# Stores of z, of the kept rows and of the first w1 and w2 operands issued by ScalarE in place of GpSimd

## The chip, the cores and the metric

The kernel runs on one core of a Trainium2 chip. The metric is the device time of one execution in microseconds, the median of several runs. Before the change the median of 3 runs is 1948.03 us (1947.04 to 1948.57).

The engines are named as in the profile: PE is TensorE (PEld its weight loads), DVE VectorE, ACT ScalarE, POOL GpSimd and SP SyncE. An engine carries out its own instructions in order. A DMA transfer is an instruction on one engine's queue (SPq, ACTq, POOL); the transfer itself then runs beside the engines.

## What is computed

A block of a network with modulation, an FNet mixing and an MLP, in float32, with S = 2048 rows and D = 1024 columns, F = 3584:

```
mod = (silu(c) @ w_mod)  ->  sa, ca, ga, sb, cb, gb
h = layernorm(x) * (1 + ca) + sa
a = h @ dft_hid_re^T ; b = h @ dft_hid_im^T
x = x + ga * (dft_seq_re @ a - dft_seq_im @ b)
h = layernorm(x) * (1 + cb) + sb
x = x + gb * (gelu(layernorm(h) @ w1 + b1) @ w2 + b2)
```

## The kernel before

Every matrix product is carried out in fp16 with each float32 operand split into a high and a low half (ScalarE makes the high half, VectorE subtracts it for the low half) and three products per pair (`PASSES`). All large products use Winograd's (Strassen's) scheme of seven products for a 2 by 2 block of matrices; `ORDER` = 0, 1, 2, 4, 3, 6, 5 is their order. Their operands are sums and differences of quarters, split into halves, and many are stored to DRAM once and loaded again later.

The stages, by the time in the profile:

- To about 617 us: normalising x, the product along the sequence, first plain (line 1272), then Winograd (line 1324). Its result u is split and stored to DRAM (line 906, issued by ScalarE), as are the operands s (line 774) and dc (line 985).
- 617 to 918 us, `gemm2`, line 1561: the product along the hidden dimension for eight blocks of 256 rows (b = 0 to 7). One product is two pieces of 12 matmuls. An eviction of a finished product to SBUF is done by ScalarE (line 1577) or VectorE (line 1583); a later product of the same bank goes on accumulating after it. Beside this VectorE and ScalarE do the two layer norms of the blocks (`ln_tasks`), whose result with gb*b2 added is the "kept" row block that is stored to the output (line 1427). The normalised rows are transposed on TensorE (line 1463) and `z_tasks` makes from them the seven operands z of a block (high half line 401, low half line 411, sums line 426), which are stored to zc in DRAM (line 1495). Weight operands of the MLP are made meanwhile: w1 for its first three groups g (line 1160) and w2 for its first pair v = 0 (line 1207), stored to DRAM through two staging buffers.
- 918 us to the end: the MLP, 28 groups of the first layer (`gemm3`, line 1755; 12 matmuls a product, evicted by line 1777 on ScalarE and 1781 on VectorE, gelu in line 1774) and 14 pairs of the second (`gemm4`, line 1864; evicted by line 1900 on ScalarE in the first pair of each half and by line 1910 on VectorE). The z of blocks 6 and 7 and the kept rows of block 7 are still being made in the first groups, from about 937 to 1000 us. SP loads the stored operands back: zc at line 1503, the stored w1 at lines 1736, 1741 and 2050, the first w2 at line 2072.

The order of all instructions is planned by the program itself when it is built. Work is cut into `Task`s with an engine, a modelled cost in us, dependencies and a due time, put in streams, and `fill_to` and `pick` hand out the next task by modelled clocks of the engines (`clk`) and modelled times at which results are there (`done`). `need` and `emitted` force what must come first. A store goes through `store`. By default it is a task of the kind "st": it takes no engine's modelled time, is issued 0.3 us (`BEHIND`) after what it stores is ready, plus the lag of its stream, and lands after `LANDS["st"]` = 4.0 us, also for z. If its ring is in the table `SYNC`, the store is a task of ScalarE with the cost given there, is put in a stream of its own with a due time ahead of all others, and lands after `SLAND` = 5.5 us:

```
        if ring in SYNC:
            t.eng, t.cost = "act", SYNC[ring]
            LANDS[t.key] = SLAND
        push(f"q_{ring}" if ring in SYNC else ring, tag or f"st_{ring}", [t], -1e6)

    SYNC = {"u": 0.5, "s": 0.8, "d": 0.8}
    SLAND = 5.5
```

The rings here are "z" (the operands z, with five or four staging places a block), "x2" (the kept rows) and "w1" (the staged w1 and w2). A task that writes a staging place again depends on the store that last read it (`slot`, `reuse`).

GpSimd's other work in these stages is the all-reduce over partitions in the norms of the weights (line 1064) and, late in the kernel, the stores that add to the output (lines 1938 and 1963).

Of the kernel before, what the change touches and what calls it, by code (L numbers as in the profile page):

```python
# [36 lines left out]
def kernel(ctx, tc, x, cre, cim, dre, dim, w1, b1, w2, b2, c, wm, out):  # L37
# [13 lines left out]
    pe, act, dve, gp, sp = nc.tensor, nc.scalar, nc.vector, nc.gpsimd, nc.sync  # L51
# [144 lines left out]
    w1_d = [dram.tile([P, 7, 2, 512], F16, tag=f"w1_{g}", name=f"w1_{g}") for g in range(14)]  # L196
    w2_d = [dram.tile([P, 7, 2, 2, 512], F16, tag=f"w2_{v}", name=f"w2_{v}") for v in range(7)]
# [67 lines left out]
    def push(stream, tag, tasks, due=0.0):  # L265
        for t in tasks:
            t.tag, t.due, t.lag = tag, due, LAGS.get(stream, LAT)
            streams.setdefault(f"st_{stream}" if t.eng == "st" else stream, deque()).append(t)

    def store(ring, n, f, after, tag=None):  # L270

        t = Task("st", 0.0, f, [after], ("st", ring, n))
        if ring in SYNC:
            t.eng, t.cost = "act", SYNC[ring]
            LANDS[t.key] = SLAND
        push(f"q_{ring}" if ring in SYNC else ring, tag or f"st_{ring}", [t], -1e6)

    SYNC = {"u": 0.5, "s": 0.8, "d": 0.8}
    SLAND = 5.5

    def slot(ring, n):
# [649 lines left out]
    dst = [0]  # L931
# [152 lines left out]
    def two1(g, n):  # L1084

        return at(raw1_at(g, n), 1024).rearrange("p (s x) -> p s x", s=2)
# [38 lines left out]
    def w1_tasks(g):  # L1125
        def after(n):
            if g < 3:
                return
            if n < 2:
                load_w1(g + 1, n + 2)  # L1130
            else:
                load_w1(g + 2, n - 2)

        s, p, sid = g % 2, g % NPAIR, {}

        def q(n):
            return two1(g, n[0]) if isinstance(n, tuple) else raw1(g, n)

        def span(m):
            return slice(m[0], m[1] + 1) if isinstance(m, tuple) else slice(m, m + 1)  # L1140

        def outs(m):
            v, n = w1c[:, span(m), s], 1 + isinstance(m, tuple)
            if g > 4:
                reuse("w1k", (g - 2, m))
            if g < 3:
                stage[0] += 1
                reuse("w1", stage[0] - 2)
                sid[m] = stage[0]
                v = at((172, 176)[stage[0] % 2], 1024 * n, F16).rearrange("p (m a x) -> p m a x", m=n, a=2)  # L1150
            return v[:, :, 0], v[:, :, 1], v

        def q1(n):
            t = q(n)
            return t if isinstance(n, tuple) else t.rearrange("p (m x) -> p m x", m=1)

        def post(m, o):

            ring, n, tag = ("w1", sid[m], "st_w1") if g < 3 else ("w1k", (g, m), None)
            store(ring, n, lambda: (gp if g < 3 else sp).dma_start(w1_d[g][:, span(m)], o[2]), ("w1", g, span(m).start), tag)  # L1160

        return left_tasks(
            q1, outs, s1c[:, p : p + 1], False, lambda n: ("raw1", g, n), lambda m: ("w1", g, m), after, post,
            (lambda m: ("g3", g - 2, m)) if g > 2 else None,
            (lambda m: slot("w1", lambda: stage[0] - 1)) if g < 3 else None,
        )
# [24 lines left out]
    def w2_tasks(v):  # L1191
        u, sid = v % 7, {}

        def outs(m):
            w = w2c[:, m]
            if v > 1:
                reuse("w2k", (v - 1, m))
            if v == 0:
                stage[0] += 1
                reuse("w1", stage[0] - 2)  # L1200
                sid[m] = stage[0]
                w = at((172, 176)[stage[0] % 2], 2048, F16).rearrange("p (s a x) -> p s a x", s=2, a=2)
            return w[:, :, 0], w[:, :, 1], w

        def post(m, o):
            ring, n, tag = ("w1", sid[m], "st_w2") if v == 0 else ("w2k", (v, m), None)
            store(ring, n, lambda: (sp if v else gp).dma_start(w2_d[v][:, m], o[2]), ("w2", v, m), tag)

        return right_tasks(
            [raw2(v, q) for q in range(4)], outs, s2c[:, u : u + 1], 1024,  # L1210
            lambda n: ("raw2g" if v == 6 else "raw2", v, n), lambda m: ("w2", v, m), (lambda q: load_w2(v + 1, q)) if v else None, post,
            (lambda m: ("g4", v - 1, m)) if v else None,
            (lambda m: slot("w1", lambda: stage[0] - 1)) if v == 0 else None,
        )
# [151 lines left out]
    def ln_tasks(b):  # L1366

        y, w, cl = yb(b), wb(b), lns[b % 2]
        su, nm, v, ve, r, a = (cl[:, n, :] for n in range(6))
# [54 lines left out]

        def keep(n):
            dve.tensor_tensor(y[:, n], y[:, n], gbb_t, op=ALU.add)
            store("x2", 2 * b + n, lambda: gp.dma_start(out[2 * b + n], y[:, n]), ("kept", b, n))

        t = two(lambda n: dve.scalar_tensor_tensor(y[:, n], y[:, n], m1[:, 3:4], ga_t, op0=ALU.mult, op1=ALU.mult), 1.2)
        t = [t[0], *two(add_x)[:1], t[1], *two(add_x)[1:]]  # L1430
# [14 lines left out]
        for n in (1, 0):  # L1445
            f = lambda n=n: act.activation(w[:, n], w[:, n], AF.Identity, scale=r[:, n : n + 1], bias=nm[:, n : n + 1])
            t.append(Task("act", 1.13, f, [k], ("w", b, n)))
        if b < NB - 1:
            n = len(two_)
# [26 lines left out]
    def z_tasks(b):  # L1476

        e, o = zt(b, 0), zt(b, 1)
        q = [e[:, 0:512], o[:, 0:512], e[:, 512:1024], o[:, 512:1024]]
        places = [O_K + 8 + 2 * k for k in range(4)] if b == NB - 1 else [152, 154, 46 if b == NB - 2 else 182, 216, 218]  # L1480
        h, k = divmod(b, 4)
        n, at_ = [0], {}

        def outs(m):
            at_[m] = n[0]
            reuse("z", (b, n[0] - len(places)) if n[0] >= len(places) else None)
            if n[0] < len(places) and 0 < b < NB - 1:
                need(f"z{b - 1}")
            v = at(places[n[0] % len(places)], 1024, F16).rearrange("p (a x) -> p a x", a=2)
            n[0] += 1  # L1490
            return v[:, 0], v[:, 1], v

        def post(m, o_):
            dst = zc_d[h][m][:, :, k].rearrange("p a c t -> p a (c t)")
            store("z", (b, at_[m]), lambda: gp.dma_start(dst, o_[2]), ("z", b, m), f"z{b}")

        return right_tasks(
            q, outs, None, 512, lambda j: ("zt", b, j % 2), lambda m: ("z", b, m), post=post,
            free=lambda m: slot("z", lambda: (b, n[0] - len(places))),
        )  # L1500
# [133 lines left out]
    for tb in range(1, NTB):  # L1634
# [3 lines left out]
        for m in ORDER:  # L1638
            for kp in range(4):
                n = opn(tb, m, kp)  # L1640
# [34 lines left out]
    for n, (name, t) in enumerate(zip(("ga", "sb", "cb", "gbb"), (ga_t, sb_t, cb_t, gbb_t))):  # L1675
        f = lambda t=t, name=name[:2]: sp.dma_start(t, row_d[name][0].partition_broadcast(P))
# [365 lines left out]
    for kind, k in seq:  # L2042
        if kind == 3:
            g = k
# [3 lines left out]
            if g == 0:  # L2048
                for m in ORDER:
                    f = lambda m=m: sp.dma_start(w1c[:, m, 0], w1_d[2][:, m])  # L2050
# [6 lines left out]
            elif g == 1:  # L2057
# [9 lines left out]
                for n in range(2):  # L2067
                    f = lambda n=n: sp.dma_start(raw1(4, n), w1[4, :, PLACE.index(n), :])
                    push("l1", "l1_4", [Task("dma", 0.75, late(f), was, ("raw1", 4, n))], due[3, 3] - 20.0)
                t = []  # L2070
                for m in ORDER:
                    f = lambda m=m: sp.dma_start(w2c[:, m], w2_d[0][:, m])
# [30 lines left out]
        else:  # L2103
            v = k
            gemm4(v, hook(v))
            if v < NV - 1:
                g = 2 * v + 2
# [56 lines left out]
```

## Time and profile before

| what | value |
| --- | --- |
| median of 3 runs | 1948.03 us |
| the profiled execution's own time | 1947.17 us |
| its span, first to last instruction | 1945.2 us |
| mean granted clock of TensorE | 0.999 |
| TensorE busy | 1931.0 us, 99% of the span, 8979 matmuls |
| VectorE busy | 1440.1 us, 74% |
| ScalarE busy | 838.3 us, 43% |
| GpSimd busy | 115.2 us, 6%, 171 instructions |
| transfers | 413.44 MB, mean 213 GB/s |

Busy time does not count the instructions that issue transfers, except on GpSimd, where the issue of a transfer is shown as the engine's work. A group's line gives the line of the program, the engine, the operation, what is written from what, how often, then busy us and the mean of one in ns, and then the idle time of that engine just before, with what ended it. A row of the waits gives who waited for whom, the total in us, how often and the longest. The chain that ended last is followed back from the last instruction to what released each step.

### The profile page before, as it was taken

To read this page: it belongs to the slowest core of one execution; us is meant where nothing else is said; L and a number is where in the kernel's file an instruction comes from. 1 tells how busy PE (TensorE), PEld (TensorE's weight loads), DVE (VectorE), ACT (ScalarE), POOL (GpSimd) and SP (SyncE) were. 2 spreads that over 40 slices of the span, in tenths; PEclk is the share of its full clock that TensorE was granted. 3 is DMA by queue.
4 is the path that set the end of the run, shared out by engine and by line. 5 is a ranking of instruction groups with operands and counts; after the bars stand their busy time and mean duration, and the time that the engine had idled before them with its cause. 6 is when DMAs were issued, how large, how long until landed. Compare 5 with 4: busy or idle time off the path is not lost.

```text
span 1945.2 us, 23621 instructions
## 1 busy us (share of the span) xinstructions
PE 1931.0 (99%) x8979; PEld 880.5 (45%) x8979; DVE 1440.1 (74%) x1872; ACT 838.3 (43%) x1081; POOL 115.2 (6%) x171
## 2 busy tenths in 40 slices
PE   9999999999999999999999999999999999999998
PEld 3444444444444444444444444444444444444443
DVE  8888879979964677876789998988862454554566
ACT  7434324544422355644676656645423412312311
POOL 0010000000001022221110000000010000000000
PEclk9999999999999999999999999999999999999999
DMA  9498897796889867778466355535665432432323
GB/s 340 161 349 250 281 359 235 253 349 230 276 289 362 329 246 258 284 269 326 170 229 219 132 176 189 175 111 184 237 202 145 141 101 63 140 103 65 109 76 87
DMA packets 149990, 413.44 MB, mean 213 GB/s; under 512 B 17146, under 2 KB 17210, under 8 KB 145788
## 3 DMA queue, kind: packets, MB, share of 16 engines
q1 hardware_dynamic: 115972, 316.75, 47.9%
q0 software_dynamic: 13024, 42.74, 7.5%
q10 hardware_dynamic: 20880, 52.44, 7.0%
q8 instruction: 70, 1.15, 0.2%
q14 instruction: 44, 0.36, 0.1%
HBM read 272.40 MB, written 135.30 MB: 210 GB/s over the span
## 4 chain that ended last, share of the span: by engine, by line
PE 85%; DVE 2%; DMA 1%; ACT 1%; issue 0%; SPq 0%; DVEq 0%
PE ps L1755 25%; PE ps L1864 25%; PE ps L1324 19%; PE ps L1561 15%; PE ps L1463 1%; DMA arena<-s 0%; DVE arena L1910 0%; DVE arena L413 0%; ACT arena L401 0%; DMA arena<-w 0%; DVE arena L1954 0%; DVE arena L518 0%; DVE arena L426 0%; ACT arena L1900 0%; DVE arena L904 0%
## 5 line engine op out<-in xcount | busy, mean ns | idle before, releaser
L1864 PE MATMUL ps<-arena 128*128 128x512 f16 x2352 | 511.0, 379 | 2.2 <-DVE arena L1910 0.9
L1755 PE MATMUL ps<-arena 128*128 128x512 f16 x2352 | 510.2, 379 | 1.2 <-ACT arena L1777 1.2
L1324 PE MATMUL ps<-arena 128*128 128x512 f16 x2016 | 435.6, 379 | 2.3 <-DMA arena<-s 2.3
L1864 PEld LDWEIGHTS <-arena 128*128 128x128 f16 x2352 | 229.9, 98 | 280.8 <-issue 1.8
L1755 PEld LDWEIGHTS <-arena 128*128 128x128 f16 x2352 | 230.2, 98 | 278.6 <-issue 1.4
L1910 DVE SCALAR_TENSOR_TENSOR arena<-ps,i4c,arena 128x1024 f32<-128x1024 f32 x179 | 229.4, 1282 | 143.1 <-PE ps L1864 140.7
L1324 PEld LDWEIGHTS <-arena 128*128 128x128 f16 x2016 | 197.1, 98 | 240.7 <-DMA arena<-s 3.5
L1561 PE MATMUL ps<-arena 128*128 128x512 f16 x1344 | 292.4, 379 | 0.0
L401 ACT ACTIVATE arena<-arena,shc 128x512 f16<-128x512 f32 (+1 forms) x115 | 116.0, 1017 | 264.2 <-PE ps L1864 175.9
L1561 PEld LDWEIGHTS <-arena 128*128 128x128 f16 x1344 | 131.5, 98 | 155.7
L790 ACT ACTIVATE arena<-arena 128x1024 f16<-128x1024 f32 x99 | 103.2, 1052 | 199.2 <-PE ps L1324 119.7
L426 DVE TENSOR_TENSOR arena<-arena 128x512 f32<-128x512 f32 (+1 forms) x228 | 171.2, 753 | 4.3
L1272 PE MATMUL ps<-arena 128*128 128x512 f16 x768 | 168.3, 382 | 2.6 <-DVE arena L793 2.0
L413 DVE SCALAR_TENSOR_TENSOR arena<-arena,shc 128x512 f16<-128x512 f32 (+1 forms) x115 | 128.2, 1122 | 50.8 <-ACT arena L401 49.9
L793 DVE SCALAR_TENSOR_TENSOR arena<-arena 128x1024 f16<-128x1024 f32 x99 | 120.0, 1220 | 41.8 <-ACT arena L790 38.5
L1774 ACT ACTIVATE arena<-arena,b1s,i1c 128x512 f32<-128x512 f32 x84 | 68.3, 813 | 149.6 <-DVE arena L1781 149.6
L1781 DVE TENSOR_TENSOR arena<-arena,ps 128x512 f32<-128x512 f32 x84 | 57.5, 685 | 94.9 <-PE ps L1755 94.5
L1272 PEld LDWEIGHTS <-arena 128*128 128x128 f16 x768 | 75.1, 98 | 95.9 <-issue 4.5
L901 ACT ACTIVATE arena<-arena 128x1024 f16<-128x1024 f32 x56 | 58.3, 1051 | 79.3 <-DMA u<-arena 40.4
L904 DVE TENSOR_TENSOR arena<-arena 128x1024 f16<-128x1024 f32 x56 | 68.0, 1219 | 22.3 <-ACT arena L901 22.3
L401 ACT ACTIVATE arena<-arena,s1c 128x512 f16<-128x512 f32 (+1 forms) x70 | 60.9, 885 | 52.6 <-DVE arena L426 34.5
L413 DVE SCALAR_TENSOR_TENSOR arena<-arena,s1c 128x512 f16<-128x512 f32 (+1 forms) x70 | 66.6, 959 | 5.7 <-ACT arena L401 5.6
(161 smaller groups left out, 1305.0 us busy)
## 6 DMA issues: line engine op xcount, KB each, us to landing
w<-arena SPq DMA_DIRECT2D x64, 512.0 KB, 4.6
arena<-w SPq DMA_DIRECT2D x119, 256.0 KB, 2.6
u<-arena ACTq DMA_DIRECT2D x56, 512.0 KB, 6.0
arena<-u SPq DMA_DIRECT2D x112, 256.0 KB, 4.1
arena<-w SPq DMA_DIRECT2D x56, 512.0 KB, 3.4
arena<-in_wm_dram SPq DMA_DIRECT2D x48, 512.0 KB, 4.9
arena<-s SPq DMA_DIRECT2D x48, 512.0 KB, 6.6
arena<-in_cim_dram SPq DMA_DIRECT2D x32, 512.0 KB, 7.4
```

Of the source, the lines that this page charges most:

```text
L401: act.activation(o[m][0], q(j), AF.Copy, **sc)
L413: dve.scalar_tensor_tensor(o[m][1], q(j), scale, o[m][0], op0=ALU.mult, op1=ALU.subtract)
L426: dve.tensor_tensor(q(d), q(a), q(b), op=op)
L790: h = Task("act", 0.96, lambda: act.activation(o[:, :, 0], s2, AF.Copy, scale=SC), list(deps) + free)
L793: dve.scalar_tensor_tensor(o[:, :, 1], s2, SC, o[:, :, 0], op0=ALU.mult, op1=ALU.subtract)
L1272: pe.matmul(bank_of(d_), hleft(d_, s, kp, a), cop(n)[:, s, b], start=(kp == 0 and s == 0 and a == 0 and b == 0), stop=(kp == 7 and s == 1 ...
L1324: pe.matmul(bank_of(st + ch), left, cop(n)[:, s, b], start=(start and kp == 0 and s == 0 and a == 0 and b == 0), stop=(kp == 3 and s == 1 ...
L1561: pe.matmul(bank_of(bk), up(N)[:, c_, a], dp(n)[:, c_, w], start=(start and ri == 0 and c_ == 0 and i == 0), stop=(ri == 1 and c_ == 3 and ...
L1755: pe.matmul(ps.rearrange("p (k t) -> p k t", k=4), w1c[:, m, s, a, d * P : (d + 1) * P], zc(m)[:, b, :, d, :], start=(start and d == 0 and ...
L1774: act.activation(dst, src, AF.Gelu_apprx_tanh, scale=inv, bias=b1s[:, 2 * p + j : 2 * p + j + 1])
L1864: pe.matmul(t[:, j], hidc[:, c_, m, a, k * P : (k + 1) * P], w2c[:, m, c_, w], start=(start and c_ == 0 and n == 0), stop=(c_ == 1 and n = ...
L1910: lambda: dve.scalar_tensor_tensor(dst, ps[b], inv, dst, op0=ALU.mult, op1=ALU.add), kp[b],
```

## The change

Four issues of stores move from GpSimd's queue to ScalarE's, and their three rings are entered in the table `SYNC`, so that the planner treats them as ScalarE's work:

```
-    SYNC = {"u": 0.5, "s": 0.8, "d": 0.8}
+    SYNC = {"u": 0.5, "s": 0.8, "d": 0.8, "z": 0.4, "x2": 0.5, "w1": 0.4}
...
-            store(ring, n, lambda: (gp if g < 3 else sp).dma_start(w1_d[g][:, span(m)], o[2]), ("w1", g, span(m).start), tag)
+            store(ring, n, lambda: (act if g < 3 else sp).dma_start(w1_d[g][:, span(m)], o[2]), ("w1", g, span(m).start), tag)
...
-            store(ring, n, lambda: (sp if v else gp).dma_start(w2_d[v][:, m], o[2]), ("w2", v, m), tag)
+            store(ring, n, lambda: (sp if v else act).dma_start(w2_d[v][:, m], o[2]), ("w2", v, m), tag)
...
-            store("x2", 2 * b + n, lambda: gp.dma_start(out[2 * b + n], y[:, n]), ("kept", b, n))
+            store("x2", 2 * b + n, lambda: act.dma_start(out[2 * b + n], y[:, n]), ("kept", b, n))
...
-            store("z", (b, at_[m]), lambda: gp.dma_start(dst, o_[2]), ("z", b, m), f"z{b}")
+            store("z", (b, at_[m]), lambda: act.dma_start(dst, o_[2]), ("z", b, m), f"z{b}")
```

What is stored, and where, stays the same. As the planner now gives these stores time on ScalarE and a later landing, the order of other instructions after the first of them can come out differently.

## The prediction

> **What bounds the kernel now.** I read the busy time by stretch first, because the page's shares are means over stages with different limits. The columns are the stretch in us, its length, then the busy time of each engine.
>
> ```profile
> 617.00:915.00 298.00, 298.00 (x1432) 141.40 (x1431) 212.78 (x374) 145.59 (x222) 53.35 (x86) 1.00 0.79 285
> 915.00:978.00 63.00, 61.84 (x303) 29.71 (x302) 42.28 (x92) 40.27 (x57) 6.41 (x10) 1.00 0.61 220
> 978.00:1014.00 36.00, 35.34 (x164) 15.86 (x163) 29.11 (x48) 25.27 (x36) 6.28 (x9) 1.00 0.71 243
> 1014.00:1940.00 926.00, 924.47 (x4282) 418.52 (x4281) 637.37 (x769) 357.94 (x455) 21.06 (x27) 1.00 0.44 139
> 1940.00:1945.20 5.20, 0.77 (x4) 0.16 (x2) 1.02 (x2) 0.00 (x0) 0.00 (x0) 0.99 0.55 203
> ```
>
> TensorE is busy in all 298 us of the stage in which most of the moved stores lie, at a granted clock of 1.00. Its gaps come later: 63.00 − 61.84 = 1.16 us, 36.00 − 35.34 = 0.66 us, 926.00 − 924.47 = 1.53 us, and 4.43 us after the last product, which is the last eviction and its store. The waits of TensorE from 617 us on name them (total us, times, longest):
>
> ```profile
> PE ps L1755 <- ACT arena L1777: 1.2, 1, 1.2
> PE ps L1864 <- DVE arena L1910: 0.9, 1, 0.9
> PE ps L1864 <- ACT arena L1900: 0.7, 2, 0.4
> PE ps L1864 <- ACT arena L401: 0.3, 1, 0.3
> PE ps L1864 <- DVE arena L413: 0.2, 1, 0.2
> ```
>
> Nothing here waits for GpSimd or for a store. The waits sum to 3.3 us, so 3.3 us is the most that any order of the other engines can give back from 617 us on. It is 0.17% of the 1947.17 us of the profiled execution. The smallest difference that a measurement of this kernel can tell from no change is taken as 0.2%, 3.9 us.
>
> **What is moved.** These groups leave GpSimd (count, then busy us and mean ns):
>
> ```profile
> L1495 POOL DMA_DIRECT2D zc<-arena x56 | 39.1, 724 | 173.3 <-DVE arena L411 144.4 <-issue 16.4 <-DVE sums L1060 8.0
> L1427 POOL DMA_DIRECT2D out_dram<-arena x16 | 8.8, 551 | 16.8 <-DVE arena L1426 11.9 <-DVE lns L1380 3.9 <-ACT arena L401 0.8
> L1160 POOL DMA_DIRECT2D w<-arena x15 | 8.2, 549 | 52.3 <-DVE arena L413 43.4 <-ACT arena L1446 3.5 <-issue 3.4
> L1207 POOL DMA_DIRECT2D w<-arena x7 | 3.9, 550 | 21.3 <-DVE arena L413 14.0 <-ACT arena L1473 7.3
> ```
>
> That is 56 + 16 + 15 + 7 = 94 stores and 60.0 us of GpSimd. GpSimd stands idle most of the time and TensorE never waits for it, so taking them away is worth nothing by itself. The all-reduces of the weight norms (L1064) and the accumulating stores of the output, which stay on GpSimd, no longer queue behind stores; as no wait of TensorE leads to them, I count 0.
>
> ScalarE gets 94 issues. Its queue already issues the stores of u and s; these rows give the time of an issue on that queue and of the wait ahead of it (ns, least, median, most):
>
> ```profile
> L906 ACTq DMA_DIRECT2D u<-arena x56: 326/326/428, 107.6 to 648.1; - x56
> L906 ACTq EVENT_SEMAPHORE  x39: 17/17/5052, 106.3 to 648.0; - x39
> L774 ACTq DMA_DIRECT2D s<-arena x32: 326/448/1682, 99.1 to 207.4; - x32
> ```
>
> So an issue costs ScalarE between 0.33 and 1.68 us. I take 0.33 to 0.45, the two medians; most of the moved stores are, like those of u, single contiguous or two-part rows sent alone. A rule that speaks against the change belongs here: the Trainium skill, Perfetto Trace Analysis, section "DMA Instruction — HWDGE (DVE, Sync)", says that the semaphore wait and the exclusive lock on the descriptor generator are spent on the issuing sequencer before it is free. The trace agrees as far as the 1.682 us of one s store and the 5.052 us of one wait go; if every issue met the lock so, the 1.1 us below would become about 1.1 × 1.68 / 0.4 = 4.6 us.
>
> **The stage of the up-products, 617 to 915 us.** 78 of the 94 stores lie here: six blocks of seven z, seven pairs of kept rows, 22 operands. They add 78 × 0.33 = 25.7 to 78 × 0.45 = 35.1 us to 145.59, so ScalarE goes from 49% of 298 us to 57 to 61%. What waits behind a store on ScalarE is the eviction L1577 and the high-half splits L401. The eviction takes 0.60 us (ns, least, median, most):
>
> ```profile
> L1577 ACT ACTIVATE arena<-ps x32: 575/597/599, 623.5 to 918.3; 128x512 f32<-128x512 f32 x32
> ```
>
> Two pieces of the chain that ended last give the pace of TensorE (start, length, matmuls):
>
> ```profile
> 685.06 5.18 PE ps L1561 x24
> ...
> 915.69 2.59 PE ps L1561 x12
> ```
>
> A product that goes on accumulating in an evicted bank comes one other product (24 matmuls, 5.18 us) after it, so the eviction may start 5.18 − 0.60 = 4.58 us late. Three stores in a row are 1.0 to 1.4 us. The trace has the same case already, with stores of u ahead of L1577 in this stage:
>
> ```profile
> 630.51 1.06 ACT L901 ACTIVATE arena<-arena 128x1024 f16<-128x1024 f32 x1 [5.46 <-DMA u<-arena]
> 632.86 0.33 ACTq L906 DMA_DIRECT2D u<-arena  x1
> 633.23 0.60 ACT L1577 ACTIVATE arena<-ps 128x512 f32<-128x512 f32 x1 [1.66 <-DVE arena L904]
> ```
>
> ScalarE stood 5.46 us for a landing, then issued a store, then evicted, and TensorE lost nothing. So this part costs 0; without that cover a held eviction would cost what it exceeds 4.58 us by.
>
> **The passage to the MLP, 937 to 1000 us.** The other 16 stores lie here: seven z of block 6, two kept rows of block 7, seven z of block 7. A product is now 12 matmuls, 2.59 us, and these evictions stand behind the stores:
>
> ```profile
> L1777 ACT ACTIVATE arena<-ps x84: 572/597/598, 920.9 to 1895.7; 128x512 f32<-128x512 f32 x84
> L1900 ACT ACTIVATE arena<-ps,i4c x16: 1093/1114/1115, 980.9 to 1522.7; 128x1024 f32<-128x1024 f32 x16
> ```
>
> Their room is 2.59 − 0.60 = 1.99 us and 2.59 − 1.11 = 1.48 us. GpSimd issued the first of these stores here, which says when their subtractions on VectorE were done:
>
> ```profile
> 944.25 1.41 POOL L1495 DMA_DIRECT2D zc<-arena  x2 [29.74 <-DVE arena L411]
> 949.10 1.41 POOL L1495 DMA_DIRECT2D zc<-arena  x2 [3.44 <-DVE arena L411]
> 954.56 0.69 POOL L1495 DMA_DIRECT2D zc<-arena  x1 [4.04 <-DVE arena L411]
> 964.38 1.42 POOL L1495 DMA_DIRECT2D zc<-arena  x2 [9.13 <-DVE arena L411]
> ```
>
> The first four cost nothing: ScalarE has a hole just behind them, which ends at
>
> ```profile
> 951.05 0.81 ACT L1774 ACTIVATE arena<-arena,b1s,i1c 128x512 f32<-128x512 f32 x1 [2.77 <-DVE arena L1781]
> ```
>
> and 4 × 0.45 = 1.8 us fit into its 2.77 us. The fifth comes due at 954.56, inside the chain that ends last, which runs over ScalarE there and ends in TensorE's 1.16 us gap:
>
> ```profile
> 954.30 1.17 ACT arena L1446
> 955.48 0.66 issue
> 956.13 1.15 ACT arena L401
> ```
>
> One issue more in it makes the gap longer by 0.33 to 0.45 us; I take 0.4. The sixth and seventh z and the two kept rows come after 964 us, where ScalarE has part of the 63.00 − 40.27 = 22.7 us free; of their 4 × 0.45 = 1.8 us between none and all lies on the way to the first down-product, and I take 0.3, nearer to none, since no gap of TensorE lies there before 982. The seven z of block 7 add 2.3 to 3.2 us to a stretch where ScalarE has 36.00 − 25.27 = 10.7 us free; the two gaps behind L1900 (0.7 in sum) lie there, and I let one store fall ahead of one of them, 0.4 us. **Sum:** 0 + 0.4 + 0.3 + 0.4 = 1.1 us, bounded from below by −3.3 and from above by the first rival.
>
> **Landing.** The loads of the second-layer operands on SP (L2072) wait for block 6's z stores to land, so the landing counts too (last column, median us from issue to landing):
>
> ```profile
> u<-arena ACTq DMA_DIRECT2D x56, 512.0 KB, 6.0
> zc<-arena POOLq DMA_DIRECT2D x56, 256.0 KB, 4.3
> ```
>
> The loads themselves, from the timeline, and the first down-product, from the chain:
>
> ```profile
> 964.41 9.65 SPq L2072 DMA_DIRECT2D arena<-w  x7
> ```
>
> ```profile
> 976.62 1.73 PE ps L1864 x9
> ```
>
> By these medians a landing goes from 4.3 to 6.0 us and those loads start 1.7 us later, from 964.41; the first down-product runs at 976 us and takes one operand in each 2.59 us, against 9.65 / 7 = 1.4 us per load. It is hidden.
>
> The profiled execution took 1947.17 us for a span of 1945.20, and the median of the three runs is 0.86 us above it. The sum goes on both alike: 1948.27 in the terms of the profile, and 1948.03 + 1.1 = 1949.1 us as the forecast.
>
> **Rivals.** *First, slower: the queue of ScalarE holds an eviction.* GpSimd could stand at a store for 29.74 or 9.13 us at no price. ScalarE takes its instructions in order too, and the planner places a store by modelled times; where VectorE is late against the plan, ScalarE stands and L1777 or L1900 behind it overruns 1.99 or 1.48 us. Against it: the median wait ahead of a u store was 17 ns, and the stand of 5.46 us shown above did not reach TensorE. For it: these rooms are less than half of the 4.58 us that one had. By price: the 16 stores form about eight groups; if three of them overrun by 2 us each, two fifths of the longest wait seen, it is 6 us, 1954.0 us. It decides from about two overruns. Chance 0.15.
>
> *Second, the better side: GpSimd's issues have been in VectorE's way.* If VectorE were held while GpSimd writes descriptors, up to 60.0 us of VectorE would come free and its subtractions and additions behind TensorE's gaps would end earlier; the gaps before 1014 us (1.16 + 0.66) would go, 1948.03 − 1.8 = 1946.2 us. The subtraction whose result is stored speaks against it:
>
> ```profile
> L411 DVE TENSOR_TENSOR arena<-arena x56: 680/684/693, 695.4 to 997.4; 128x512 f16<-128x512 f32 x56
> ```
>
> All 56 took the same to 2%, beside a GpSimd that issued for 60 us in that time. The Trainium skill, SBUF — State Buffer, section "SBUF: two separate sides", has such an exclusive lock between the two engines, for some VectorE operations; this row shows none of it. The stalls can also go by a luckier order alone. Chance 0.12.
>
> *Third, the order moves elsewhere.* The planner charges ScalarE 0.4 or 0.5 us per store and waits 5.5 us for a landing where it had 4.0, so every later choice may differ, up to the end. One or two new gaps of the size of the present ones (1.2 us) without the old ones going would give 1.1 + 2.4 = 3.5 us, 1951.5 us. Chance 0.10.
>
> **How the numbers follow.** The forecast has 0.63, with 1947.5 to 1950.5 for itself: its bounds of issue price, and the spread of the runs of before. The range runs from 1946.1, the second rival, to 1952.6, past the third; it leaves out about 0.05 below and 0.13 above. Slower by over 0.2% (above 1951.9) takes the first rival and a part of the third: 0.18. Faster by over 0.2% (below 1944.1) would need more than all the gaps that can go: 0.03. No change: 0.79.
>
> **What would show it.** Right: GpSimd without L1495, L1427, L1160 and L1207; 94 issues on ScalarE's queue with a median near 0.33 to 0.45 us; TensorE again 298 of 298 us up to the passage; in the passage a gap behind L1777 of about 1.6 us. Wrong: a wait of TensorE for L1577 in the stage before; several waits behind L1777 or L1900 of 1 to 3 us, with a long wait ahead of a store on ScalarE just before; issues of over 1 us as a rule; or L411 shorter than 0.68 us.

## The result

The changed kernel takes 1960.51 us (median of 4 runs, 1959.10 to 1962.62) where the kernel before took 1947.62 on the same chip (4 runs): the ratio is 1.0063 (95% interval 1.0051 to 1.0075). It is slower by about 12.9 us. The forecast was 1949.1 with a range up to 1952.6, so the time lies 7.9 us beyond that range. The profiled execution took 1960.46 us for a span of 1958.7, 13.5 us more than the span of 1945.2 before. Two single executions far above the rest, 5037.86 us in the run cost50 and 3434.37 us in the run behind, are in none of the ratios below.

The moved instructions themselves came out nearly as priced. On ScalarE's queue after the change (ns, least, median, most):

```profile
L1495 ACTq DMA_DIRECT2D zc<-arena x56: 520/527/1046, 694.9 to 1008.2; - x56
L1495 ACTq EVENT_SEMAPHORE  x50: 17/17/3615, 694.3 to 1007.4; - x50
L1427 ACTq DMA_DIRECT2D out_dram<-arena x16: 333/344/755, 674.1 to 972.5; - x16
L1160 ACTq DMA_DIRECT2D w<-arena x15: 326/332/1396, 675.0 to 787.2; - x15
L1207 ACTq DMA_DIRECT2D w<-arena x7: 326/333/372, 818.0 to 864.7; - x7
```

By medians that is 56 × 0.527 + 16 × 0.344 + 15 × 0.332 + 7 × 0.333 = 42.3 us of ScalarE, the upper end of 94 × 0.33 to 94 × 0.45. Added up one by one the 94 issues take 47.0 us, since some are longer than the medians. Only the z stores are dearer by the median than either median taken. The longest wait ahead of a store is 3.6 us. An issue does not always keep ScalarE from its work: it can lie beside an instruction that is still running, as in this pair, behind which the next instruction starts at 961.91 us, about when the split ends:

```profile
960.87 1.14 ACT L401 ACTIVATE arena<-arena,shc 128x1024 f16<-128x1024 f32 x1
960.89 0.52 ACTq L1495 DMA_DIRECT2D zc<-arena  x1
```

Of the 47.0 us 14.0 lie beside running instructions in this way. GpSimd's busy time goes from 115.2 to 53.9 us, and nothing of VectorE gets faster for it:

```profile
L411 DVE TENSOR_TENSOR arena<-arena x56: 680/684/693, 694.2 to 1007.5; 128x512 f16<-128x512 f32 x56
```

TensorE's longest waits from 617 us on are now these (total us, times, longest). The 1.2 us behind L1777 and 0.9 of the 4.1 us behind L1910 were there before, the others are new:

```profile
PE ps L1864 <- DVE arena L1910: 4.1, 4, 1.5
PE ps L1864 <- ACT arena L1900: 3.5, 1, 3.5
PE ps L1561 <- DMA arena<-u: 2.7, 1, 2.7
PE ps L1755 <- ACT arena L1777: 1.2, 1, 1.2
```

By stretch, TensorE is idle for 926.00 − 920.74 = 5.26 us in the last long row (1.53 before), and the granted clock is below 1.00 in two rows:

```profile
617.00:915.00 298.00, 297.96 (x1428) 141.01 (x1426) 212.20 (x379) 145.23 (x221) 4.64 (x7) 1.00 0.80 281
915.00:978.00 63.00, 59.14 (x274) 27.50 (x275) 36.13 (x74) 32.98 (x46) 0.00 (x0) 0.97 0.70 245
978.00:1014.00 36.00, 32.45 (x152) 15.29 (x151) 25.76 (x44) 22.36 (x29) 0.67 (x1) 0.95 0.41 132
1014.00:1940.00 926.00, 920.74 (x4260) 416.17 (x4258) 640.53 (x780) 368.45 (x473) 17.88 (x26) 1.00 0.44 140
```

**Where the 13.5 us lie.** TensorE does the same products in both kernels, so the starts of the same piece can be set side by side. TensorE's timeline before (start, length, matmuls), the last up-product, the first piece of the MLP, the second pair of first layers, the second pair of second layers and what follows it:

```profile
915.53 2.75 PE L1561 MATMUL ps<-arena 128*128 128x512 f16 x12
918.12 18.29 PE L1755 MATMUL ps<-arena 128*128 128x512 f16 x84
...
1013.69 36.42 PE L1755 MATMUL ps<-arena 128*128 128x512 f16 x168
...
1122.55 36.42 PE L1864 MATMUL ps<-arena 128*128 128x512 f16 x168
1158.81 16.57 PE L1755 MATMUL ps<-arena 128*128 128x512 f16 x76
```

The same places after, with the gaps between them:

```profile
917.70 4.45 PE L1561 MATMUL ps<-arena 128*128 128x512 f16 x12 [2.74 <-DMA arena<-u]
922.86 18.29 PE L1755 MATMUL ps<-arena 128*128 128x512 f16 x84
...
990.08 32.78 PE L1864 MATMUL ps<-arena 128*128 128x512 f16 x144 [3.55 <-ACT arena L1900]
1023.17 36.42 PE L1755 MATMUL ps<-arena 128*128 128x512 f16 x168 [0.32 <-ACT ps L1052]
...
1132.22 5.34 PE L1864 MATMUL ps<-arena 128*128 128x512 f16 x24
1139.02 10.53 PE L1864 MATMUL ps<-arena 128*128 128x512 f16 x48 [1.46 <-DVE arena L1910]
1150.66 7.93 PE L1864 MATMUL ps<-arena 128*128 128x512 f16 x36 [1.11 <-DVE arena L1910]
1159.22 13.18 PE L1864 MATMUL ps<-arena 128*128 128x512 f16 x60 [0.63 <-DVE arena L1910]
1172.24 2.97 PE L1755 MATMUL ps<-arena 128*128 128x512 f16 x13
```

The offset is 922.86 − 918.12 = 4.74 us, then 1023.17 − 1013.69 = 9.48, then 9.67, then 13.43, and it stays there to the end. So there are three places:

- **The last up-product, near 917 us:** a gap of 2.74 us for an operand from DRAM, and the 12 matmuls behind it take 4.45 us where they took 2.75: 4.4 of the 4.74 us. The rest lies in no gap or slow piece that these rows show.
- **The first down-products, near 990 us:** a gap of 3.55 us behind the eviction L1900, 144 matmuls in 32.78 us (31.24 where nothing slows them, as in late_only below), and 0.32 us, less the 0.23 and 0.43 us of gaps that stood there before: 4.7 us.
- **The second pair of down-products, near 1140 us:** three gaps behind L1910, 3.2 us, and 5.34 + 10.53 + 7.93 + 13.18 = 36.98 us of pieces for 36.42: 3.8 us.

By the profile none of these waits is directly for a store on ScalarE's queue. Three theories were put to the test. **A**: transfers of SP and ScalarE take turns on one set of eight completion semaphores in the built program and GpSimd's have their own, so the moved stores hold up SP's loads. **B**: the issue is harmless and the order that the planner makes from the new table is worse. **C**: ScalarE stands at a store with an eviction behind it (the first rival).

### The profile page after: what moved, and what is told of

Same layout as the page of the kernel before. It is cut to its first block, busy times and chain, and to the rows that moved or that the text cites. A ratio compares the mean times of both kernels' runs of the same rounds, so it can differ in the third digit from the quotient of the medians.

```text
span 1958.7 us, 23528 instructions
## 1 busy us (share of the span) xinstructions
PE 1934.4 (99%) x8979; PEld 880.6 (45%) x8979; DVE 1440.4 (74%) x1872; ACT 838.3 (43%) x1081; POOL 53.9 (3%) x77
## 4 chain that ended last, share of the span: by engine, by line
PE 77%; DVE 5%; DMA 3%; ACT 1%; issue 1%; SPq 0%; DVEq 0%; ACTq 0%
PE ps L1755 23%; PE ps L1864 21%; PE ps L1324 18%; PE ps L1561 13%; DVE arena L413 2%; DMA arena<-in_w_dram 1%; DMA arena<-s 1%; DVE arena L426 1%; ACT arena L401 1%; DVE arena L1910 1%; PE ps L1463 1%; DMA out_dram<-arena 0%; DMA arena<-u 0%; DVE arena L1781 0%; DMA zc<-arena 0%
## 5 line engine op out<-in xcount | busy, mean ns | idle before, releaser
L1910 DVE SCALAR_TENSOR_TENSOR arena<-ps,i4c,arena 128x1024 f32<-128x1024 f32 x179 | 229.5, 1282 | 143.4 <-PE ps L1864 139.0
```

The costliest lines, as they stand in the source:

```text
L1910: lambda: dve.scalar_tensor_tensor(dst, ps[b], inv, dst, op0=ALU.mult, op1=ALU.add), kp[b],
```

## The experiments

**The queue alone and the plan alone.** queue_only moves the four issues and leaves the table; plan_only has the table and leaves the issues on GpSimd. The orders of TensorE, VectorE and SP are those of the kernel before in the first, and those of the changed kernel in the second.

```
queue_only: before, with act for gp in the four stores, and
    SYNC = {"u": 0.5, "s": 0.8, "d": 0.8}
plan_only: before, with gp in the four stores, and
    SYNC = {"u": 0.5, "s": 0.8, "d": 0.8, "z": 0.4, "x2": 0.5, "w1": 0.4}
```

> The four stores are issued by ScalarE, but the planner's table is as before, so TensorE, VectorE and SyncE have exactly the order of before and ScalarE has that order with 94 issues in it. Theory A (shared completion semaphores: the transfers of SyncE and ScalarE take turns on one set of eight, each waits for the eighth transfer before it to land, so a load on SyncE waits for a store on ScalarE to be computed and to land): slower than before by 3 to 8 us, with a wait of TensorE for a load of an up-operand or of weights near 900 to 920 us, and SyncE waiting there for landings of z or of kept rows. Theory B (the new order of the plan): within 1 us of before. Theory C (ScalarE held at a store in front of an eviction): slower, with waits of TensorE for L1577, L1777 or L1900 and no late load.

> The planner's table is that of the changed kernel, but GpSimd issues the stores, so TensorE, VectorE and SyncE have exactly the order of the changed kernel and its ScalarE order without the 94 issues. Theory A: no late load at 905 to 918 us, so about 4.6 us less than the changed kernel, and nearly the time of before if all of the loss is from the shared semaphores. Theory B: the loss of 13 us stays, within 2 us. Theory C: the time of before within 2 us. If the loss is in parts, the gap of 3.5 us ahead of the first down-product (waiting for L1900) and the three at 1139 to 1159 us stay here and the late load goes: about 8 us slower than before.

queue_only: 1947.47 us, ratio 0.9993 (0.9983 to 1.0002). plan_only: 1962.96 us, ratio 1.0073 (1.0058 to 1.0088). The whole loss comes with the table and none with the queue: B holds, A and C fall. Nor does relief of GpSimd show in either. TensorE's waits in queue_only are those of before, with 0.6 us more behind L1777, 0.2 us more behind L1910 and 0.2 us for an operand u. They sum to 4.3 us where they were 3.3:

```profile
PE ps L1755 <- ACT arena L1777: 1.8, 2, 1.2
PE ps L1864 <- DVE arena L1910: 1.1, 2, 0.9
...
PE ps L1561 <- DMA arena<-u: 0.2, 1, 0.2
```

What A describes does exist, only it is not the cause. In the trace's records the transfers of SP and ScalarE count up the same eight semaphores and those of GpSimd eight others, and the load of the late operand waits for the one that a kept-row store counts up. So in the chain of the changed kernel it is issued when that store has landed; in plan_only, where stores and loads can't meet so, the load is issued 9.9 us earlier and takes 17.81 us to land. First the changed kernel, then plan_only:

```profile
902.19 7.77 DMA out_dram<-arena
...
909.98 7.67 DMA arena<-u
```

```profile
900.12 17.81 DMA arena<-u
```

**One ring, or the other two.**

```
z_alone: act and SYNC only for the ring "z"
no_z:    act and SYNC only for the rings "x2" and "w1"
```

> Only the 56 stores of z move to ScalarE, in queue and table; kept rows and operands stay on GpSimd. Theory A: the load that came 10 us late was held by a store of kept rows (and the one before it by a z), so without the kept rows the late load is nearly on time: 3 to 5 us less than the changed kernel. Theory B: z is the larger part of the moved work in the passage, so most of the 8 us after 918 us stay. Theory C: 7 of the 9 us of the passage stay.

> Only the kept rows and the first w1 and w2 operands move, in queue and table; z stays on GpSimd. Theory A: few transfers of ScalarE among the loads from 885 to 918 us (two kept rows), so SyncE waits for at most one of them and the time is that of before within 2 us. Theory B: another order again, between 0 and 8 us slower. Theory C: within 1 us of before, since the seven z of blocks 6 and 7 are not on ScalarE.

z_alone: 1957.45 us, ratio 1.0046 (1.0031 to 1.0061). no_z: 1960.65 us, ratio 1.0064 (1.0047 to 1.0081). Each loses most of it or all, and both show the wait for the operand and the gaps behind L1910 near 1140 us; the gap behind L1900 near 990 us is only in z_alone, at 1.6 us. no_z has two gaps that the changed kernel has not: 2.52 us at the first down-products behind another line of ScalarE (L1052), and 1.98 us behind L1910 near 1060 us. The losses of the parts do not add up to the loss of the whole.

**The early stores, or the late ones.** The table applies to the three rings only up to the end of the up-products, or only from there on; all four issues are on ScalarE.

```
-        if ring in SYNC:
+        if ring in SYNC and (ring in ("u", "s", "d") or in_order[0]):        # late_only: not in_order[0]
...
-        push(f"q_{ring}" if ring in SYNC else ring, tag or f"st_{ring}", [t], -1e6)
+        push(f"q_{ring}" if t.eng == "act" else ring, tag or f"st_{ring}", [t], -1e6)
```

> The four stores are on ScalarE's queue. The new table holds for the stores that are handed out up to 918 us; the 16 after that are planned as in the kernel before. TensorE's order is then the one of the changed kernel, VectorE's leaves it only at the end of the up-products. Theory B1 (each gap of TensorE belongs to the order at its own place): the wait for the up operand of about 2.7 us near 917 and the slower matmuls behind it stay, 4 to 5 us, the waits behind L1900 near 990 and L1910 near 1140 go: about 1952.5 us, ratio 1.0025. Rival B2 (the new order of 617 to 918 us puts the layer norms and the z of blocks 6 and 7 late, and the later gaps are its consequence): all three gaps stay, about 1960.5 us, ratio 1.006. Rival B3 (only the late stores matter, the operand's wait is a chance of the transfers): same as before, 1948 us.

> The four stores are on ScalarE's queue. The new table holds only for the 16 stores that are handed out after 918 us, so that all engines keep the order of the kernel before up to there. Theory B1 (each gap belongs to the order at its own place): no wait for an up operand, the waits behind L1900 and L1910 come, 4.6 + 3.9 us: about 1956.5 us, ratio 1.0045. Rival B2 (the later gaps follow from the order before 918 us): no loss, 1948 us, ratio 1.000. A value between, with one of the two late gaps alone, would be near 1952 us.

early_only: 1955.57 us, ratio 1.0036 (1.0023 to 1.0049). late_only: 1950.33 us, ratio 1.0011 (1.0002 to 1.0021). B3 falls. B1 is right for two places: with the early stores planned anew the wait for the operand comes, though at 2.12 us and without slow matmuls behind it, and with the late ones the gap behind L1900, though with 1.8 us it is half of what B1 expected. For the third place B2 is right and B1 is not: the gaps near 1140 us come with the early stores too, when the late ones are planned as before. late_only has a gap of 2.08 us behind L1910 too, but one pair of down-products earlier, near 1058 us. In early_only, then late_only:

```profile
919.22 2.76 PE L1561 MATMUL ps<-arena 128*128 128x512 f16 x12 [2.12 <-DMA arena<-u]
...
1133.31 10.53 PE L1864 MATMUL ps<-arena 128*128 128x512 f16 x48 [1.46 <-DVE arena L1910]
1145.58 7.93 PE L1864 MATMUL ps<-arena 128*128 128x512 f16 x36 [1.74 <-DVE arena L1910]
```

```profile
982.48 31.24 PE L1864 MATMUL ps<-arena 128*128 128x512 f16 x144 [1.80 <-ACT arena L1900]
```

**Which entry of the plan.** The table does three things to a store: it gives it time on ScalarE, precedence there, and a later landing.

```
landing_only: queue_only with LANDS ("st","x2"), ("st","w1"), ("st","z") = 5.5 in place of 4.0
cost0:        the changed kernel with "z": 0.0, "x2": 0.0, "w1": 0.0 in SYNC
land4:        the changed kernel with LANDS[t.key] = 4.0 for the three rings
cost0_land4:  both
```

> The four stores are on ScalarE's queue but stay out of the table; only their landing is planned as 5.5 us where it was 4.0. Theory B4 (the later landing frees the staging places later in the plan and so puts the operands late): most of the loss, 1956 us or more, ratio 1.004 or more. Rival B5 (ScalarE's modelled time and the precedence of a store on it reorder the rest): no loss or a small one, 1948 to 1951 us.

> The changed kernel with costs of 0.0 for the three rings; the landing of 5.5 us stays. Theory B8 (cost alone): within 0.2% of before. Rival B9 (landing): a loss of 3 us or more, at least the 3.8 us that the landing cost where the stores were planned as before. VectorE's busy time from 917 to 1016 us goes with it, as above.

> The changed kernel with the landing of the three rings planned as 4.0 us, as before; the costs of 0.4 and 0.5 us on ScalarE stay. Theory B8 (the cost alone displaces the layer norms and the z): the loss stays over 5 us, ratio 1.003 or more. Rival B9 (it takes the later landing as well, which frees the staging places later): within 0.2% of before. In both, if the missing work of VectorE is what counts, VectorE's busy time from 917 to 1016 us goes with the loss: about 72 us without a loss, 62 to 67 us with one.

> The changed kernel with the cost of the three rings set to 0.0 and their landing to 4.0 us as before, so that what is left of the table is that the stores are ScalarE's tasks, due ahead of all others, without the lag of their streams. Theory B5 (the modelled time that ScalarE loses is what reorders): most of the loss goes, 1948 to 1951 us. Rival B6 (precedence alone is enough, since a store that is due soon holds ScalarE's other tasks back in the plan): the loss stays, 1956 us or more, ratio 1.004 or more. Rival B7 (any other order than the one before costs 5 to 13 us, whatever its cause): this one and the landing alone both lose over 5 us, at other places.

landing_only: ratio 1.0023 (1.0013 to 1.0032). cost0: 1.0043 (1.0028 to 1.0058). land4: 1.0058 (1.0041 to 1.0075). cost0_land4: 1.0003 (0.9993 to 1.0012). Precedence alone costs nothing, though all engines' orders differ from those of before: B6 and B7 fall. The cost in the plan and the later landing are each enough for most of the loss once the store is ScalarE's task. So B8 missed cost0 and B9 missed land4, and neither is the whole cause; the landing by itself, with the stores planned as before, gave 1952.5 us, between what B4 and B5 expected. The places differ as well. land4 has the three of the changed kernel. cost0 has the wait for the operand, and in place of the other two a gap of 4.49 us at the first down-product, which waits there for its weights (loaded by L2072):

```profile
984.23 33.95 PE L1864 MATMUL ps<-arena 128*128 128x512 f16 x144 [4.49 <-DMA arena<-w]
```

landing_only has one at another place again, 3.57 us at the transposes L1463 near 917 us. The measured landing of z is 4.1 us, where the new table says 5.5 and the old entry 4.0; the issues take 0.33 to 0.53 us, where the table says 0.4 and 0.5. So for the z, 56 of the 94 stores, the figures of land4 are nearer to the measured ones than those of the new table. For the kept rows, which land after 6.2 us, they are not. Both lose, and cost0_land4, which says that the stores cost ScalarE nothing, does not.

**Size, or chance.** land4 with other costs; and the kernel before, stores on GpSimd, with one constant of the plan changed.

```
cost25, cost50, cost150: land4 with "z", "x2", "w1" at 0.1, 0.125, 0.1; 0.2, 0.25, 0.2; 0.6, 0.75, 0.6
behind: the kernel before with BEHIND = 0.8 in place of 0.3
```

> The changed kernel with the landing planned as 4.0 us and a quarter of the modelled costs (0.1 and 0.125 us a store). Theory F (the loss grows with the modelled cost): a quarter of the loss, 1.5 us above none, ratio 1.0015 to 1.002. Rival G (the loss jumps with the order that comes out; TensorE's order is here that of neither neighbour): anything from none to 1.006, by which of the three gaps are there: the wait for the up operand, the one behind L1900 and those behind L1910.

> The same with half of the costs (0.2 and 0.25 us). TensorE's order is that of the full costs. Theory F: half of the loss, ratio 1.003. Rival G: as with the full costs, ratio 1.005 to 1.0065, with the same three gaps.

> The same with one and a half of the costs (0.6 and 0.75 us), and another order of TensorE again. Theory F: one and a half of the loss, ratio 1.008 to 1.009. Rival G: no rule, 1.000 to 1.009, with gaps at other places or the same.

> The kernel before, its stores on GpSimd and its table untouched; only the constant by which the plan puts a store of GpSimd or SP behind what it stores goes from 0.3 to 0.8 us, which changes the order of all engines from the stage of the up-products on. Rival G in its widest form (the order before is a lucky one and most other orders cost): a loss of over 3 us, ratio 1.002 or more. Theory F (it is ScalarE's modelled time that costs): within 0.2% of before.

| costs in the plan | 0 | a quarter | half | full | one and a half |
| --- | --- | --- | --- | --- | --- |
| ratio | 1.0003 | 1.0006 | 1.0060 | 1.0058 | 1.0130 |

The intervals are 0.9997 to 1.0016 for the quarter, 1.0040 to 1.0081 for the half and 1.0115 to 1.0146 for one and a half; behind has 1.0010 (1.0000 to 1.0020). This is no line: the loss steps up between a quarter and a half, where the order of TensorE becomes that of land4, and with one and a half a single gap makes nearly all of it, behind the same loads L2072:

```profile
1002.19 38.15 PE L1864 MATMUL ps<-arena 128*128 128x512 f16 x168 [21.40 <-DMA arena<-w]
```

Theory F falls and G holds as far as steps go. In its widest form G falls too: behind and cost0_land4 displace the order on all engines at a price of at most 0.2%. Both still have a wait of 1.5 us for the operand u; it is the other two places that they spare.

**Is it VectorE's missing work?** Between 917 and 1016 us VectorE is busy for 72.0 us before and 61.8 after. lo_twice gives the kernel queue_only 9.5 us more to do there.

```
-                    dve.tensor_tensor(o[m][1], q(j), o[m][0], op=ALU.subtract)
+                    [dve.tensor_tensor(o[m][1], q(j), o[m][0], op=ALU.subtract) for _ in range(1 if in_order[0] else 2)]
```

> The four stores on ScalarE's queue with the order of the kernel before, and every subtraction (L411) of the z of blocks 6 and 7 done twice with the same result: 14 more of 0.68 us, 9.5 us of VectorE between about 938 and 1000 us. This is about the work of VectorE that the changed kernel lacks there (61.8 us from 917 to 1016 where before had 72.0). Theory D (VectorE has too little room behind the passage, so that what it lacks there comes back as gaps of TensorE behind L1910 near 1140 us, whatever the order): gaps behind L1910 of 3 to 6 us near 1140 and a loss of 5 to 10 us in all, 1953 to 1958 us. Rival (the gaps at 1140 come from the order in which the weights are prepared there): no gap near 1140, a loss of at most 3 us, 1948 to 1951 us.

1954.79 us, ratio 1.0035 (1.0022 to 1.0048). The size is as theory D has it, the place is not: there is no gap near 1140 us. TensorE pays at once, in the passage (two of its gaps):

```profile
955.16 7.93 PE L1755 MATMUL ps<-arena 128*128 128x512 f16 x36 [1.05 <-DVE arena L1781]
965.48 9.62 PE L1755 MATMUL ps<-arena 128*128 128x512 f16 x36 [2.39 <-ACT arena L1777]
```

So theory D falls. What it shows is how little room the passage has: 9.5 us more of VectorE raise the gaps from 917 to 1016 us from 2.4 to 6.3 us, and 36 matmuls take 9.62 us for 7.93. That VectorE does less there in the changed kernel may be a consequence of the gaps as well as a cause.

**One load put back.** The last up operand came late beside a load of 1 MB (x rows of block 7, L1535), which waits for the transposes of block 5. On SP's queue, before and after:

```profile
883.81 0.38 SPq L1535 DMA_DIRECT2D arena<-in_x_dram  x1
```

```profile
895.16 0.38 SPq L1535 DMA_DIRECT2D arena<-in_x_dram  x1
```

After, it is issued among the seven pairs of loads of zc and w1, where the transfer engines are busy all the time: from 910 to 925 us their share is 1.03 to 1.06. It was 1.01 to 1.03 before as well, so what differs is which loads share it. xw_behind issues this load behind the last up operand and leaves the order of the other engines as it is.

```
in load_xw, for block 7: no issue; in load_up, behind the last operand:
+            N == NP * NB - 1 and sp.dma_start(wb(7), x[14:16].rearrange("r p e -> p r e"))
```

> The changed kernel with nothing but one load moved on SP's queue: the 1 MB of x rows of block 7 are issued behind the last up operand, not ahead of the last two; the order of the other engines stays. Theory E (the last up operand lands late because that load, displaced by the late transposes of block 5, now takes transfer time ahead of it): the wait L1561 <- u of 2.7 us and the slow matmuls behind it go, 4 to 5 us less, about 1956 us, ratio 1.0040, unless the rows of x come late for VectorE, which would show as a wait of DVE L1415. Rival (the seven zc and w1 loads alone fill the transfers): the wait stays, 1960 us, ratio 1.006.

1957.52 us, ratio 1.0053 (1.0038 to 1.0068). The wait for the operand and the slow matmuls behind it are gone: TensorE is busy for 300.00 of the 300 us from 617 to 917. The gap of 3.5 us behind L1900 and those behind L1910 stay. So it is that load which makes the operand late there, as theory E has it. One thing moves along with it: the last two up operands are issued at 898.94 and 908.23 us, where the changed kernel issues them at 905.59 and 909.98. An earlier issue alone is not the cure, since plan_only issues them at 897.31 and 900.12 us, with the 1 MB ahead of them, and has the wait all the same. By the medians the time falls by 3 us rather than 4 to 5, and the intervals of the two ratios overlap. The trace says where the rest went: from the start of the up-products to that of the MLP it takes 4.6 us less, but behind the gap at L1900 144 matmuls take 34.14 us where they took 32.78, and the gaps behind L1910 are 0.7 us longer. Nothing else is cured by it.

**The second place in the trace.** ScalarE's rows ahead of the first L1900 show it. Before, the last two splits of the second group's operands (scale shc) come straight behind the eviction of block 7's transposes (L2034):

```profile
975.78 1.96 ACT L2034 ACTIVATE arena<-ps 128x1024 f32<-128x1024 f32 x2
977.63 1.75 ACT L401 ACTIVATE arena<-arena,shc 128x512 f16<-128x512 f32 x2
980.86 1.11 ACT L1900 ACTIVATE arena<-ps,i4c 128x1024 f32<-128x1024 f32 x1 [1.47 <-issue]
```

After, two splits for z of block 7 (no scale) have gone ahead of them:

```profile
980.51 1.94 ACT L2034 ACTIVATE arena<-ps 128x1024 f32<-128x1024 f32 x2
982.34 1.15 ACT L401 ACTIVATE arena<-arena,shc 128x1024 f16<-128x1024 f32 x1
983.38 1.15 ACT L401 ACTIVATE arena<-arena 128x512 f16<-128x512 f32 x2
985.57 1.88 ACT L401 ACTIVATE arena<-arena,shc 128x512 f16<-128x512 f32 x2 [1.04 <-DVE arena L426]
988.91 1.11 ACT L1900 ACTIVATE arena<-ps,i4c 128x1024 f32<-128x1024 f32 x1 [1.47 <-DVE i4c L1845]
```

From the end of L2034 to L1900 it is 3.1 us before and 6.5 after. That this order comes from the modelled cost of the late stores is argued from the gap's presence in the changed kernel, plan_only, land4, cost50 and xw_behind (3.5 us each), late_only and z_alone (1.8 and 1.6), and its absence, or at most 0.4 us, where those costs are missing (early_only, no_z, cost0, cost0_land4) or a quarter (cost25). In cost150 TensorE's gap of 21.4 us takes its place. The absence says less in no_z and cost0, where TensorE has another gap at the first down-products (2.52 us behind L1052 and 4.49 us for weights). No run puts back these splits alone, and why late_only has half of the gap is open.

**What stays open.** The gaps near 1140 us come with early stores planned at half the costs or at the full ones; at a quarter and at one and a half there are none. There the product of two scales (i4c, L1845) that L1910 needs stands behind a row of operand work on VectorE. Before, it came 1.0 us after the start of this pair of down-products (1122.55 us), after the change 5.2 us after it (1132.22 us). Before, then after:

```profile
1123.56 0.15 DVE L1845 TENSOR_TENSOR i4c<-i4c,ihc 128x1 f32<-128x1 f32 x1
```

```profile
1137.42 0.15 DVE L1845 TENSOR_TENSOR i4c<-i4c,ihc 128x1 f32<-128x1 f32 x1
```

VectorE is busy for 93% of the 109 us ahead of this pair in both kernels, so it is no busier than before, and what differs is the order of its work. Which displaced task puts L1845 there was not followed.

## Why the prediction was wrong

- **The bound and the room above it** were right: TensorE sets the end, and no part of the change could give back more than 3.3 us. None gave back anything.
- **The issues on ScalarE** were nearly right: 42.3 us by the medians, none as long as the 1.68 us that one s store took, and the stage from 617 to 915 us takes them at no price (queue_only). The gap expected behind L1777, 1.6 us, stayed at 1.2 us in the changed kernel and in queue_only, where the fifth z store is issued at 954.49 us beside running instructions. The 0.4 us behind L1900 did not come either (0.7 us in all before and in queue_only). What came in queue_only is a second gap behind L1777, 0.6 us where the sum had 0.3, and 0.2 us each behind L1910 and for an operand u, where it had nothing. So its waits are 1.0 us longer in all, and that this meets the sum of 1.1 us is luck. In the time of queue_only not even this is to be seen: by the interval queue_only lies between 3.3 us below and 0.4 us above before. The hole named for the first four z of block 6 begins at 948.28 us, behind the 944.25 us of the first two, so it was room for the other two alone.
- **The landing** was right in its result, as the first down-product does not wait for L2072, and wrong in its figure. The z land after 4.1 us, not after the 6.0 of the u (4.3 before), and the loads L2072 start at 960.88 us where they started at 964.41, not 1.7 us later. In cost0 and cost150 the first down-product does wait for them, by 4.5 and 21.4 us: "It is hidden" holds for the order before, not for any order.
- **The first rival** (an eviction held by a store) fell: waits ahead of a store reach 3.6 us, and queue_only loses nothing.
- **The second rival** (GpSimd in VectorE's way) fell: L411 takes 0.684 us with and without it.
- **The third rival, "the order moves elsewhere"**, is what happened, and here is the step that failed. The sum 0 + 0.4 + 0.3 + 0.4 has no term for the new order: it counted it at nothing, while the text said that every later choice may differ. The rival that did price it took "One or two new gaps of the size of the present ones (1.2 us)", 2.4 us. There are five new gaps at three places, 2.74 + 3.55 + 1.46 + 1.11 + 0.63 = 9.5 us, and a small one of 0.32. Their size is not that of the present gaps. It is the time that a task comes late when its place in a queue changes: an operand 2.7 us, a split and a scale 3.5 us. On top come 1.70 and 1.54 us of slow matmuls behind the two long gaps, for which neither the sum nor the rival had a term.

What could have been read beforehand is where an order has no room. From 917 to 1016 us the trace of before had the L1777 gap in the chain, the loads of zc and w1 together with the last up operands, and 1.48 to 1.99 us of room behind each eviction. With a table that changes the plan from the first moved store on, at 674 us, these places say more of the size of the third rival than the gaps of before; its chance of 0.10 was too small for a change that reorders all five queues.

## What to carry to other kernels

Before costing a moved instruction, ask whether the edit changes only the instruction or also the figures from which a scheduler orders everything else; if it does, these are two changes, and each can be timed without the other. A re-planned order is priced by the tight places that it passes (a burst of loads, an eviction with little room, an engine over 90% busy), not by the gaps that the present order happens to have. A model with truer figures does not by itself give a better order: here costs of 0.4 and 0.5 us, near to the measured 0.33 to 0.53, lost 0.6% with either landing, and "costs nothing" with the landing of before lost nothing.

## What the hardware showed

A gap of TensorE costs more than its length once it is long enough. The granted clock in 5 us stretches (the figure ahead of the last two columns) of the changed kernel, around its two long gaps:

```profile
915.00:920.00 5.00, 2.30 (x7) 0.97 (x8) 1.47 (x3) 0.00 (x0) 0.00 (x0) 0.81 1.04 407
920.00:925.00 5.00, 5.00 (x25) 2.54 (x23) 2.15 (x2) 1.62 (x2) 0.00 (x0) 0.85 1.06 433
...
990.00:995.00 5.00, 4.92 (x16) 1.95 (x16) 4.50 (x12) 1.66 (x4) 0.67 (x1) 0.68 0.17 56
```

In stretches of 0.5 us the clock is 0.50, and each time it is back at 1.00 within 5 us of the first matmul; the price is 1.70 and 1.54 us. From 617 us on, over all runs, every gap of 3.5 us or more was followed by it, at a price of 1.4 to 3.0 us, and none up to 2.12 us. Between, it came behind 2.39 (lo_twice), 2.40 (plan_only), 2.61 (cost0) and 2.74 us and did not behind 2.52 (no_z) and 2.85 us (z_alone). The Trainium skill, TensorE: Matmul & The Clock Gate, section "Part 1: The HAM clock gate (the "warmup" mystery)", has the clock fall to half after an idle window of about 3.4 us that runs free of the program. The trace agrees on the half, and that the length alone does not decide agrees with a free-running window; the losses behind gaps of 2.39 to 2.74 us came earlier than an idle window of 3.4 us would allow. Behind each of these four gaps the clock is low for 3.4 us in all (1.71 us lost at half speed), and not always from the first matmul on: in lo_twice it stands at 1.00 for another 1 us.

An issue of a z store takes ScalarE 0.527 us, where GpSimd spent 0.724 us. Stores of the other three kinds take ScalarE 0.33 to 0.34 us, where GpSimd spent 0.55 us.
